# Square root and reciprocal for the first two layer-norm chunks, second halves on Pool, two weight loads on ScalarE's queue, staged warming

## The chip, the cores and the metric

The kernel runs on one core of a Trainium2 chip. The metric is device time in microseconds (us); lower is better. "Span" is the time from the first to the last instruction in a profile; it is about 1.8 us under the time. The engines are named as the profile names them: PE is TensorE's matmuls, PEld its weight loads, DVE is VectorE, ACT is ScalarE, POOL is GpSimd, SP is the engine that issues most DMAs.

## The reference, cut to what matters

```python
x  = A_x                                  # 2048 tokens x 1024, bf16
xn = layernorm(x)                         # over the 1024 columns
out = x + attention(xn, wq, wk, wv, wo, beta) + mixer(xn, w1, b1, w2, b2)

def mixer(x, w1, b1, w2, b2):
    h = layernorm(x)                      # a second norm, of the normed x
    u = gelu(einsum('bsd,sf->bdf', h, w1) + b1)   # contraction over the 2048 tokens
    ...
```

The first matmuls of the mixer contract over tokens. So the kernel can start them as soon as the first 128 tokens ("chunk 0" of 16) are loaded, normed and scaled. This document is about the first 8 us, up to there, and about how the following chunks keep up.

## The kernel before: the parts that matter

Names used below: `xin` is x as loaded, by chunk; `ln_st`, `ln_mv`, `ln_rs` hold statistics, mean and variance, and 1/std; `h` is the scaled chunk; `w1early` is the part of w1 that the first stage uses. Loads are all issued by SP, in this order (x chunks and w1 chunks: first chunk, count):

```python
for kind, c0, n in (("x", 0, 1), ("x", 1, 1), ("x", 2, 1), ("w", 0, 2), ("x", 3, 1), ("x", 4, 2), ("w", 2, 2), ("x", 6, 2),
                    ("w", 4, 4), ...):
    ...
with fw.group(reads=[self.R_warm], writes=[self.R_bank[0]]):
    for _ in range(self.N_WARM):          # 10 matmuls on zeros, to warm TensorE up
        fw.mm(self.bank(0), self.warm[:, 0:P], self.warm[:], start=True, stop=True)
```

Even chunks get their statistics on VectorE (`D`, `d`), odd ones on ScalarE (`A`, second pass `A'`). `S` is 1/std: an add of eps on VectorE, then a power of -0.5 on Pool. `h` is the scaling. This list is the order of emission; each engine runs its own part of it in order.

```python
NORM_ORDER = (["D0 A1 S0 d2 h0 A1' A3 S1 d2' h1"] +
              [f"S{c} d{c + 2} h{c} A{c + 1}' A{c + 3} S{c + 1} d{c + 2}' h{c + 1}" for c in range(2, 14, 2)] + ...)

def rstd(self, c):                        # S
    fw.op("dve", lambda e: e.tensor_scalar(var, ..., E_H, op0=ALU.mult, op1=ALU.add), ...)
    fw.op("pool", lambda e: e.tensor_tensor(rs, var, self.expo[:, 0:1], op=ALU.pow), ...)

def scale_h(self, c):                     # h: chunks 0 and 1 in two halves
    for h0, h1 in ((0, 1), (1, 2)) if c < 2 else ((0, 2),):
        cols = slice(512 * h0, 512 * h1)
        self.fw.op("dve", lambda e: e.tensor_scalar(self.h[:, c, cols], self.xin[:, c, cols], self.ln_mv[:, c, 0:1],
                                                    self.ln_rs[:, c, 1:2], op0=ALU.subtract, op1=ALU.mult), ...)
```

The first stage then runs 8 matmuls per chunk: 4 that need only the first half of h, then 4 that need the second half.

The softmax here doesn't subtract the row's maximum and nothing guards it: scores larger than these inputs give would overflow.

Of the kernel before, what the change touches and what calls it, by code (L numbers as in the profile page):

```python
# [6 lines left out]
ACT = mybir.ActivationFunctionType  # L7
# [338 lines left out]
class _Kernel:  # L346
# [31 lines left out]
    def alloc(self):  # L378
        nc = self.nc
        a = self.keep = _Arena(nc, self.SB_BASE, self.SB_END)  # L380
        self.ident = a.take("ident", [P, P], BF16)
        self.brow1 = a.take("brow1", [P, 32], BF16)
        self.brow2 = a.take("brow2", [P, 32], BF16)
        self.bcol = a.take("bcol", [P, 2, 32], BF16)
        self.b1c = a.take("b1c", [P, N_FCH], F32)
        self.b2c = a.take("b2c", [P, N_TCH], F32)
        self.beta_sb = a.take("beta_sb", [P, N_HEAD], BF16)
        self.gcol = a.take("gcol", [P, N_HEAD], F32)
        self.gate = a.take("gate", [P, N_GRP, 2, 4], F32)
        self.eps8 = a.take("eps8", [P, 2, 4], F32)  # L390
        self.diag = a.take("diag", [P, 4, VW], F32)
        self.ln_st = a.take("ln_st", [P, N_TCH, 12], F32)
        self.ln_mv = a.take("ln_mv", [P, N_TCH, 2], F32)
        self.ln_rs = a.take("ln_rs", [P, N_TCH, 2], F32)
        self.expo = a.take("expo", [P, N_TCH], F32)
        self.ln_sm = a.take("ln_sm", [P, N_TCH, 1], F32)
        self.vA = [a.take(f"vA{i}", [P, 4, 16, VW], BF16) for i in range(2)]
        self.MZ32 = a.take("MZ32", [P, N_GRP, GW], F32)
        self.MZbf = a.take("MZbf", [P, N_GRP, GW], BF16)
        self.srec = a.take("srec", [P, 2, 32], F32)  # L400
        self.xnT = [a.take(f"xnT{s}", [P, N_DCH, SEG_L], BF16) for s in range(N_SEG)]
        self.gT = a.take("gT", [P, N_FCH, D_MODEL], BF16)

        self.R_ident, self.R_beta, self.R_gcol, self.R_gate = Res("ident"), Res("beta"), Res("gcol"), Res("gate")
        self.R_brow1, self.R_brow2 = [[Res(f"brow{i}_{j}") for j in range(5)] for i in range(2)]
        self.R_b1c, self.R_b2c = Res("b1c"), Res("b2c")
        self.R_eps, self.R_diag = Res("eps8"), Res("diag")
        self.R_st = [Res(f"st{c}") for c in range(N_TCH)]
        self.R_rs = [Res(f"rs{c}") for c in range(N_TCH)]
        self.R_rs0, self.R_expo = Res("rs0"), Res("expo")  # L410
        self.R_vA = [[Res(f"vA{i}_{c}") for c in range(4)] for i in range(2)]
        self.R_MZ32 = [Res(f"mz32_{g}") for g in range(N_GRP)]
        self.R_MZbf = [Res(f"mzbf_{g}") for g in range(N_GRP)]
        self.R_srec = [Res(f"srec{i}") for i in range(2)]
        self.R_xnT = [Res(f"xnT{c}") for c in range(N_TCH)]
        self.R_gT = [[Res(f"gT{fc}_{h}") for h in range(2)] for fc in range(N_FCH)]
        self.R_out = [Res(f"out{c}") for c in range(N_TCH)]

        self.early_base = a.at
        e = _Arena(nc, self.early_base, self.SB_END)  # L420
        self.xin = e.take("xin", [P, N_TCH, D_MODEL], BF16)
        self.junk = e.take("junk", [P, D_MODEL], BF16)
        self.warm = e.take("warm", [P, 512], BF16)
        self.early_end = e.at = self.early_base + 40960
        self.h = e.take("h", [P, N_TCH, D_MODEL], BF16)
        w1_at = (e.at + 31) // 32 * 32
        self.w1ring = [e.take(f"w1s{i}", [P, N_TCH, 256], BF16) for i in range(3)]
        self.w1early = nc.alloc_sbuf_tensor_at("w1early", [P, N_TCH, 512], BF16, offset=w1_at)
        self.late_end = e.at
        self.R_xin = [Res(f"xin{c}") for c in range(N_TCH)]  # L430
        self.R_junk, self.R_warm = Res("junk"), Res("warm")
        self.R_h = [[Res(f"h{c}_{h}") for h in range(2)] for c in range(N_TCH)]
        self.R_hh = [[self.R_h[c][h] for c in range(N_TCH)] for h in range(2)]
        self.R_w1s = [Res(f"w1s{i}") for i in range(3)]
# [78 lines left out]
    def consts(self):  # L513
# [5 lines left out]
        for fp in range(N_FCH // 2):  # L519
            self.w1_ring.srcs.append(self.B_w1[:, fp * 256:(fp + 1) * 256].rearrange("(c p) f -> p c f", p=P))  # L520
        self.R_w1e = [Res(f"w1e{c}") for c in range(N_TCH)]
        fw.op("act", lambda e: e.activation(self.junk[:, 0:1], self.warm[:, 0:1], ACT.Gelu_apprx_tanh),
              reads=[self.R_warm], writes=[self.R_junk])
        for kind, c0, n in (("x", 0, 1), ("x", 1, 1), ("x", 2, 1), ("w", 0, 2), ("x", 3, 1), ("x", 4, 2), ("w", 2, 2), ("x", 6, 2),
                            ("w", 4, 4), ("x", 8, 4), ("w", 8, 4), ("x", 12, 4), ("w", 12, 4)):
            if kind == "x":
                self.load_x(c0, n)
            else:
                self.fw.dma(self.w1early[:, c0:c0 + n, :],
                            self.B_w1[c0 * P:(c0 + n) * P, 0:512].rearrange("(c p) f -> p c f", p=P),  # L530
                            writes=self.R_w1e[c0:c0 + n])
        self.w1_ring.issued = 2
        for brow, src, n, R in ((self.brow1, self.B_b1, N_FCH, self.R_brow1), (self.brow2, self.B_b2, N_TCH, self.R_brow2)):
            for j in range(4):
# [1 line left out]
                       reads=[R[4]], writes=[R[j]])  # L536
        fw.dma(self.beta_sb[:], self.A_beta.partition_broadcast(P), writes=[self.R_beta])

        fw.op("pool", lambda e: e.memset(self.expo[:], -0.5), writes=[self.R_expo])
        fw.op("pool", lambda e: e.memset(self.ident[:], 0.0), writes=[self.R_ident])  # L540
        fw.op("pool", lambda e: e.affine_select(self.ident[:], self.ident[:], pattern=[[-1, P]],
                                                compare_op=ALU.not_equal, fill=1.0, base=0,
                                                channel_multiplier=1),
              reads=[self.R_ident], writes=[self.R_ident])
        with fw.group(reads=[self.R_warm], writes=[self.R_bank[0]]):
            for _ in range(self.N_WARM):
                fw.mm(self.bank(0), self.warm[:, 0:P], self.warm[:], start=True, stop=True)

    def bias_columns(self):
# [22 lines left out]
    def gates(self):  # L572
# [13 lines left out]



    NORM_ORDER = (["D0 A1 S0 d2 h0 A1' A3 S1 d2' h1"] +
                  [f"S{c} d{c + 2} h{c} A{c + 1}' A{c + 3} S{c + 1} d{c + 2}' h{c + 1}" for c in range(2, 14, 2)] +  # L590
                  ["S14 h14 A15' S15 C h15"])

    def norm_and_first_hidden(self):
        for word in " ".join(self.NORM_ORDER).split():
            kind, second = word[0], word.endswith("'")
            c = int(word[1:].rstrip("'") or 0)
            if kind == "C":
                self.bias_columns()
            elif kind in "Dd":
                self.stats_dve(c, (0, 1) if kind == "D" else (1,) if second else (0,))  # L600
            elif kind == "A":
                self.stats_act(c, second)
            elif kind == "S":
                self.rstd(c)
            else:
                self.scale_h(c)
        self.rstd_first()
        for c in range(N_TCH - 2):
            self.early_hidden(c, c + 1, (range(0, 8, 2), range(1, 8, 2)))
        self.early_hidden(N_TCH - 2, N_TCH, [(b,) for b in range(8)])  # L610
        self.late_consts()

    def stats_dve(self, c, halves):
        fw = self.fw
        src, st, R = self.xin[:, c, :], self.ln_st[:, c, :], self.R_st[c]
        for h in halves:
            fw.op("dve", lambda e: e.bn_stats(st[:, 6 * h:6 * h + 6], src[:, 512 * h:512 * h + 512]),  # L617
                  reads=[self.R_xin[c]], writes=[R])
        if halves[-1]:
            fw.op("dve", lambda e: e.bn_aggr(self.ln_mv[:, c, :], st.rearrange("p (a s) -> p a s", s=6)),  # L620
                  reads=[R], writes=[R])

    def stats_act(self, c, second):

# [9 lines left out]
    def rstd(self, c):  # L634


        fw = self.fw
        R, var, rs = self.R_st[c], self.ln_mv[:, c, 1:2], self.ln_rs[:, c, 1:2]
        fw.op("dve", lambda e: e.tensor_scalar(var, self.ln_sm[:, c, :] if c % 2 else var, 1.0 / D_MODEL if c % 2 else 1.0,
                                               E_H, op0=ALU.mult, op1=ALU.add), reads=[R], writes=[R])  # L640
        fw.op("pool", lambda e: e.tensor_tensor(rs, var, self.expo[:, 0:1], op=ALU.pow), reads=[R, self.R_expo],
              writes=[self.R_rs[c]])

    def rstd_first(self):
        fw = self.fw
# [6 lines left out]
    def scale_h(self, c):  # L652
        reads = [self.R_xin[c], self.R_st[c], self.R_rs[c]]
        for h0, h1 in ((0, 1), (1, 2)) if c < 2 else ((0, 2),):
            cols = slice(512 * h0, 512 * h1)
            self.fw.op("dve", lambda e: e.tensor_scalar(self.h[:, c, cols], self.xin[:, c, cols], self.ln_mv[:, c, 0:1],
                                                        self.ln_rs[:, c, 1:2], op0=ALU.subtract, op1=ALU.mult),
                       reads=reads, writes=self.R_h[c][h0:h1])

    def early_hidden(self, c0, c1, bank_groups):  # L660
# [433 lines left out]
```

## Time and profile before

| | before |
|---|---|
| time, first three executions | 699.26, 697.68, 697.30 (median 697.68) |
| span of the profiled execution | 695.4 us |
| PE busy | 99% |
| first real matmul | 7.09 us |
| second stage starts | 34.71 us |

First, the page's busy times by engine, and its chain of what ended last:

```profile
PE 685.7 (99%) x4746; PEld 326.5 (47%) x4830; DVE 257.2 (37%) x581; ACT 277.7 (40%) x333; POOL 100.4 (14%) x156
PE 97%; DMA 1%; issue 1%; SPq 1%; DVE 0%
```

TensorE is the limit from end to end. Where it waits, the next view shows: the waits of PE (who waited for whom: us in total, times, longest).

```profile
PE ps_all L194 <- DVE h L656: 1.4, 1, 1.4
PE ps_all L194 <- DVE brow L517: 1.3, 1, 1.3
PE ps_all L194 <- issue: 0.3, 2, 0.2
```

There are two waits that matter, both in the first 7.1 us: before the warming matmuls, and between them and the first real one. The timeline of the head (start, duration, engine, line, operation, output and inputs, count, idle time before it and who ended it):

```profile
1.25 4.45 PE L194 MATMUL ps_all<-warm 128*128 128x512 bf16 x10 [1.25 <-DVE brow L517]
4.19 1.06 ACT L627 ACTIVATE junk<-xin 128x1024 bf16<-128x1024 bf16 x1 [1.89 <-DMA xin<-in_A_x_dram]
5.29 0.15 DVE L639 TENSOR_SCALAR ln_mv<-ln_mv 128x1 f32<-128x1 f32 x1
5.53 0.55 POOL L641 TENSOR_TENSOR ln_rs<-ln_mv,expo 128x1 f32<-128x1 f32 x1 [3.96 <-DVE ln_mv L639]
5.94 0.69 DVE L617 BATCH_NORM_STATS2 ln_st<-xin 128x6 f32<-128x512 bf16 x1 [0.49 <-DMA xin<-in_A_x_dram]
6.55 0.72 DVE L656 TENSOR_SCALAR h<-xin,ln_mv,ln_rs 128x512 bf16<-128x512 bf16 x2
7.09 27.79 PE L194 MATMUL ps_all<-h,w1early 128*128 128x512 bf16 x126 [1.39 <-DVE h L656]
34.71 5.56 PE L194 MATMUL ps_all<-h,w1s 128*128 128x512 bf16 x24
```

From 7.09 to 34.71 the 128 matmuls of the first stage take 27.62 us, 0.216 us each, without a gap. (The trace misses two of their records.)

A matmul's displayed end is modelled, about 0.38 us after its start, so a displayed idle time is some 0.16 us shorter than the time lost.

### The profile page before, as it was taken

To read this page: it belongs to the slowest core of one execution; us is meant where nothing else is said; L and a number is where in the kernel's file an instruction comes from. 1 tells how busy PE (TensorE), PEld (TensorE's weight loads), DVE (VectorE), ACT (ScalarE), POOL (GpSimd) and SP (SyncE) were. 2 spreads that over 40 slices of the span, in tenths; PEclk is the share of its full clock that TensorE was granted. 3 is DMA by queue.
4 is the path that set the end of the run, shared out by engine and by line. 5 is a ranking of instruction groups with operands and counts; after the bars stand their busy time and mean duration, and the time that the engine had idled before them with its cause. 6 is when DMAs were issued, how large, how long until landed. Compare 5 with 4: busy or idle time off the path is not lost.

```text
span 695.4 us, 11228 instructions
## 1 busy us (share of the span) xinstructions
PE 685.7 (99%) x4746; PEld 326.5 (47%) x4830; DVE 257.2 (37%) x581; ACT 277.7 (40%) x333; POOL 100.4 (14%) x156
## 2 busy tenths in 40 slices
PE   8999999999999999999999999999999999999998
PEld 3444444444444444444444445444444444445454
DVE  7740000000011334333436455536445553434445
ACT  7521211111134444444455444454544444534440
POOL 2600000000001111111121211112121111121130
PEclk9999999999999999999999999999999999999999
DMA  9497684227036536645263544525273544437014
GB/s 315 110 218 175 151 224 123 77 60 140 1 133 121 109 67 131 115 109 126 47 129 95 117 95 90 129 47 137 64 150 80 97 95 73 97 64 152 9 31 137
DMA packets 210537, 77.17 MB, mean 111 GB/s; under 512 B 173112, under 2 KB 202808, under 8 KB 210488
## 3 DMA queue, kind: packets, MB, share of 16 engines
q1 hardware_dynamic: 210344, 76.42, 47.8%
q8 instruction: 38, 0.62, 0.4%
q14 instruction: 11, 0.09, 0.1%
q10 hardware_dynamic: 144, 0.03, 0.0%
HBM read 59.79 MB, written 5.24 MB: 94 GB/s over the span
## 4 chain that ended last, share of the span: by engine, by line
PE 97%; DMA 1%; issue 1%; SPq 1%; DVE 0%
PE ps_all L194 97%; DMA xin<-in_A_x_dram 1%; SPq L216 1%; DVE ln_st L617 0%; DVE fin L1051 0%; PE ps_all L200 0%
## 5 line engine op out<-in xcount | busy, mean ns | idle before, releaser
L194 PE MATMUL ps_all<-gT,w2h 128*128 128x512 bf16 x868 | 207.8, 380 | 1.6 <-issue 0.2
L811 ACT ACTIVATE pT<-ps_all 128x512 bf16<-128x512 f32 (+1 forms) x128 | 151.4, 1234 | 76.7 <-PE ps_all L194 76.7
L194 PE MATMUL ps_all<-h,w1s 128*128 128x512 bf16 x752 | 165.1, 379 | 0.8
L806 POOL TENSOR_SCALAR_AFFINE_SELECT pT<-pT 128x512 bf16<-128x512 bf16 x128 | 83.9, 680 | 557.5 <-ACT pT L811 557.5
L194 PEld LDWEIGHTS ps_all<-gT,w2h 128*128 128x128 bf16 x896 | 83.1, 98 | 105.7 <-issue 13.8
L194 PEld LDWEIGHTS ps_all<-h,w1s 128*128 128x128 bf16 x768 | 75.1, 98 | 90.6
L845 DVE CAST ost<-ps_all 128x264 bf16<-128x264 f32 (+1 forms) x128 | 49.2, 398 | 169.4 <-PE ps_all L194 169.3
L713 ACT ACTIVATE gT<-ps_all,b1c 128x512 bf16<-128x512 f32 x56 | 35.1, 687 | 142.0 <-PE ps_all L194 136.4
L755 DVE CAST kT<-ps_all 128x512 bf16<-128x512 f32 x32 | 22.0, 688 | 176.9 <-PE ps_all L194 176.9
L194 PE MATMUL ps_all<-xnT,wk 128*128 128x512 bf16 x256 | 60.5, 379 | 0.0
L194 PE MATMUL ps_all<-xnT,wq 128*128 128x512 bf16 x256 | 60.4, 378 | 0.0
L194 PEld LDWEIGHTS ps_all<-vA,pT 128*128 128x128 bf16 x1280 | 47.7, 96 | 22.6
L194 PE MATMUL ps_all<-wv_sb,xnT 128*128 128x512 bf16 x227 | 54.0, 379 | 1.6
L739 ACT ACTIVATE qT<-ps_all 128x512 bf16<-128x512 f32 x32 | 19.1, 597 | 77.8 <-PE ps_all L194 77.8
L194 PE MATMUL ps_all<-vA,pT 128*128 128x33 bf16 x1280 | 48.6, 178 | 0.0
L951 DVE SCALAR_TENSOR_TENSOR stg<-ps_all,b2c,stg 128x512 bf16<-128x512 f32 x32 | 24.0, 750 | 61.7 <-PE ps_all L194 61.6
L758 ACT ACTIVATE etmp<-kT 128x512 bf16<-128x512 bf16 x24 | 15.1, 629 | 59.0 <-DVE kT L755 59.0
L194 PEld LDWEIGHTS ps_all<-xnT,wk 128*128 128x128 bf16 x256 | 23.8, 98 | 23.1
L194 PEld LDWEIGHTS ps_all<-wv_sb,xnT 128*128 128x128 bf16 x256 | 23.5, 97 | 23.7
L194 PEld LDWEIGHTS ps_all<-xnT,wq 128*128 128x128 bf16 x256 | 23.4, 97 | 23.2
L773 ACT ACTIVATE vA<-ps_all 128x512 bf16<-128x512 f32 x32 | 19.2, 600 | 37.1 <-PE ps_all L194 37.1
L194 PE MATMUL ps_all<-qT,kT 32*128 32x384 bf16 (+3 forms) x512 | 31.9, 299 | 0.0
(70 smaller groups left out, 419.7 us busy)
## 6 DMA issues: line engine op xcount, KB each, us to landing
w2h<-in_B_w_dram SPq DMA_DIRECT2D x32, 448.0 KB, 4.8
w1s<-in_B_w_dram SPq DMA_DIRECT2D x12, 1024.0 KB, 5.8
wq<-in_A_wq_dram SPq DMA_DIRECT2D x32, 256.0 KB, 4.4
wk<-in_A_wk_dram SPq DMA_DIRECT2D x32, 256.0 KB, 5.1
stg<-in_A_x_dram SPq DMA_DIRECT2D x16, 256.0 KB, 3.0
out_dram<-stg SPq DMA_DIRECT2D x16, 256.0 KB, 2.0
xin<-in_A_x_dram SPq DMA_DIRECT2D x2, 1024.0 KB, 10.5
wv_sb<-in_A_wv_dram SPq DMA_DIRECT2D x2, 1024.0 KB, 9.0
```

What stands on the lines that cost most here:

```text
L194: ins = self.nc.tensor.matmul(*args, **kwargs)
L216: ins = es.eng.dma_start(out_ap, in_ap, transpose=True) if transpose else es.eng.dma_start(out_ap, in_ap)
L713: fw.op("act", lambda e: e.activation(self.gT[:, fc, half * 512:(half + 1) * 512], self.bank(b), ACT.Gelu_apprx_tanh, bias=self.b1c[:, fc: ...
L739: fw.op("act", lambda e: e.activation(self.qT[k][:], self.bank(b), ACT.Copy), reads=[self.R_bank[b]], writes=[self.R_qT[k]])
L755: fw.op("dve", lambda e: e.tensor_copy(self.kT[k][:], self.bank(b)), reads=[self.R_bank[b]], writes=[self.R_kT[k]])
L758: fw.op("act", lambda e: e.activation(self.etmp[1][:], self.kT[k][:], ACT.Exp), reads=[self.R_kT[k]], writes=[self.R_etmp[1]])
L773: fw.op("act", lambda e: e.activation(self.vA[i][:, c, :, 0:D_HEAD], self.bank(b).rearrange("p (h d) -> p h d", d=D_HEAD), ACT.Copy), read ...
L806: fw.op("pool", lambda e: e.affine_select(d, d, pattern=[[0, 4], [1, P]], compare_op=ALU.is_ge, fill=0.0, base=0, channel_multiplier=-1), ...
L811: self.fw.op("act", lambda e: e.activation(dst, src, ACT.Exp, scale=SCALE), reads=R_src, writes=R_dst)
L845: fw.op("dve", lambda e: e.tensor_copy(dst, self.ps[:, b, 0:n * VW]), reads=[self.R_bank[b]], writes=[self.R_ost[o][qb]])
L951: fw.op("dve", lambda e: e.scalar_tensor_tensor(dst, self.bank(b), self.b2c[:, c:c + 1], dst, op0=ALU.add, op1=ALU.add), reads=[self.R_ban ...
```

## The change

The intent is an earlier first real matmul. Chunks 0 and 1 get their 1/std by a square root on ScalarE and a reciprocal on VectorE, in place of add and Pool power. VectorE scales only their first halves; Pool takes the second halves. The first two w1 loads go out on ScalarE's queue, early. Three more warming matmuls, which wait for chunk 0's statistics, fill TensorE's idle gap. The gelu table is loaded later, in ScalarE's idle time.

```diff
-        (activation of Gelu_apprx_tanh, to load its table)
+        self.load_table(ACT.Sqrt)
-        for kind, c0, n in (("x", 0, 1), ("x", 1, 1), ("x", 2, 1), ("w", 0, 2), ("x", 3, 1), ("x", 4, 2), ("w", 2, 2), ("x", 6, 2),
+        for kind, c0, n in (("x", 0, 1), ("x", 1, 1), ("w", 0, 2), ("x", 2, 1), ("w", 2, 2), ("x", 3, 1), ("x", 4, 2),
...
-                            writes=self.R_w1e[c0:c0 + n])
+                            writes=self.R_w1e[c0:c0 + n], issuer="act" if c0 < 4 else "sp")
...
-    NORM_ORDER = (["D0 A1 S0 d2 h0 A1' A3 S1 d2' h1"] +
+    NORM_ORDER = (["D0 W0 A1 Q0 r0 h0 A1' Q1 A3 d2 e2 r1 h1 g2 S2 d4 h2 A3' A5 S3 d4' h3 V0 V1"] +
...                  # W: keep_warm(3, [R_st[c]])   Q: square root   r: reciprocal
...                  # e, g: second half of the statistics, aggregate   V: the add of eps, late   G: gelu's table
+    def std_first(self, c):
+        ... "act", activation(self.ln_rs[:, c, 1:2], src, ACT.Sqrt, bias=self.e_h[:], scale=k)
+    def rstd_of_std(self, c):
+        ... "dve", reciprocal(rs, rs)
...
-            self.fw.op("dve", lambda e: e.tensor_scalar(self.h[:, c, cols], ...
+            self.fw.op("pool" if h0 else "dve",
+                       lambda e: e.tensor_scalar(self.h[:, c, cols], ...
```

More of the change, by code (lines that the diff above doesn't have):

```diff
@@ L395, in alloc @@
         self.expo = a.take("expo", [P, N_TCH], F32)
+        self.e_h = a.take("e_h", [P, 1], F32)
         self.ln_sm = a.take("ln_sm", [P, N_TCH, 1], F32)
@@ L521, in consts @@
         self.R_w1e = [Res(f"w1e{c}") for c in range(N_TCH)]
-        fw.op("act", lambda e: e.activation(self.junk[:, 0:1], self.warm[:, 0:1], ACT.Gelu_apprx_tanh),
-              reads=[self.R_warm], writes=[self.R_junk])
-        for kind, c0, n in (("x", 0, 1), ("x", 1, 1), ("x", 2, 1), ("w", 0, 2), ("x", 3, 1), ("x", 4, 2), ("w", 2, 2), ("x", 6, 2),
-                            ("w", 4, 4), ("x", 8, 4), ("w", 8, 4), ("x", 12, 4), ("w", 12, 4)):
+        self.load_table(ACT.Sqrt)
+        for kind, c0, n in (("x", 0, 1), ("x", 1, 1), ("w", 0, 2), ("x", 2, 1), ("w", 2, 2), ("x", 3, 1), ("x", 4, 2),
+                            ("x", 6, 2), ("w", 4, 4), ("x", 8, 4), ("w", 8, 4), ("x", 12, 4), ("w", 12, 4)):
             if kind == "x":
@@ L537, in consts @@
         fw.dma(self.beta_sb[:], self.A_beta.partition_broadcast(P), writes=[self.R_beta])
-        fw.op("pool", lambda e: e.memset(self.expo[:], -0.5), writes=[self.R_expo])
+        fw.op("pool", lambda e: e.memset(self.e_h[:], E_H), writes=[self.R_expo])
+        fw.op("pool", lambda e: e.memset(self.expo[:], -0.5), reads=[self.R_expo], writes=[self.R_expo])
         fw.op("pool", lambda e: e.memset(self.ident[:], 0.0), writes=[self.R_ident])
@@ L544, in consts, with load_table, keep_warm @@
               reads=[self.R_ident], writes=[self.R_ident])
-        with fw.group(reads=[self.R_warm], writes=[self.R_bank[0]]):
-            for _ in range(self.N_WARM):
+        self.keep_warm(self.N_WARM)
+    def load_table(self, func):
+        self.fw.op("act", lambda e: e.activation(self.junk[:, 0:1], self.warm[:, 0:1], func), reads=[self.R_warm],
+                   writes=[self.R_junk])
+    def keep_warm(self, n, reads=()):
+        fw = self.fw
+        with fw.group(reads=[self.R_warm, *reads], writes=[self.R_bank[0]]):
+            for _ in range(n):
                 fw.mm(self.bank(0), self.warm[:, 0:P], self.warm[:], start=True, stop=True)
@@ L584, in gates @@
               reads=[self.R_gcol, self.R_gate], writes=[self.R_gate])
-    NORM_ORDER = (["D0 A1 S0 d2 h0 A1' A3 S1 d2' h1"] +
-                  [f"S{c} d{c + 2} h{c} A{c + 1}' A{c + 3} S{c + 1} d{c + 2}' h{c + 1}" for c in range(2, 14, 2)] +
-                  ["S14 h14 A15' S15 C h15"])
+    NORM_ORDER = (["D0 W0 A1 Q0 r0 h0 A1' Q1 A3 d2 e2 r1 h1 g2 S2 d4 h2 A3' A5 S3 d4' h3 V0 V1"] +
+                  [f"S{c} d{c + 2} h{c} A{c + 1}' A{c + 3} S{c + 1} d{c + 2}' h{c + 1}" for c in range(4, 14, 2)] +
+                  ["S14 h14 A15' G S15 C h15"])
     def norm_and_first_hidden(self):
@@ L598, in norm_and_first_hidden @@
                 self.bias_columns()
+            elif kind == "W":
+                self.keep_warm(3, [self.R_st[c]])
             elif kind in "Dd":
                 self.stats_dve(c, (0, 1) if kind == "D" else (1,) if second else (0,))
+            elif kind == "e":
+                self.stats_dve(c, (1,), False)
+            elif kind == "g":
+                self.stats_sum(c)
+            elif kind == "Q":
+                self.std_first(c)
+            elif kind == "r":
+                self.rstd_of_std(c)
+            elif kind == "V":
+                self.add_e_h(c)
+            elif kind == "G":
+                self.load_table(ACT.Gelu_apprx_tanh)
             elif kind == "A":
@@ L611, in norm_and_first_hidden, with stats_dve @@
         self.late_consts()
-    def stats_dve(self, c, halves):
+    def stats_dve(self, c, halves, sum_up=True):
         fw = self.fw
@@ L618, in stats_dve, with stats_sum @@
                   reads=[self.R_xin[c]], writes=[R])
-        if halves[-1]:
-            fw.op("dve", lambda e: e.bn_aggr(self.ln_mv[:, c, :], st.rearrange("p (a s) -> p a s", s=6)),
-                  reads=[R], writes=[R])
+        if halves[-1] and sum_up:
+            self.stats_sum(c)
+    def stats_sum(self, c):
+        st, R = self.ln_st[:, c, :], self.R_st[c]
+        self.fw.op("dve", lambda e: e.bn_aggr(self.ln_mv[:, c, :], st.rearrange("p (a s) -> p a s", s=6)),
+                   reads=[R], writes=[R])
     def stats_act(self, c, second):
@@ L634, in rstd, with add_e_h @@
     def rstd(self, c):
-        fw = self.fw
-        R, var, rs = self.R_st[c], self.ln_mv[:, c, 1:2], self.ln_rs[:, c, 1:2]
-        fw.op("dve", lambda e: e.tensor_scalar(var, self.ln_sm[:, c, :] if c % 2 else var, 1.0 / D_MODEL if c % 2 else 1.0,
-                                               E_H, op0=ALU.mult, op1=ALU.add), reads=[R], writes=[R])
-        fw.op("pool", lambda e: e.tensor_tensor(rs, var, self.expo[:, 0:1], op=ALU.pow), reads=[R, self.R_expo],
-              writes=[self.R_rs[c]])
+        self.add_e_h(c)
+        self.fw.op("pool", lambda e: e.tensor_tensor(self.ln_rs[:, c, 1:2], self.ln_mv[:, c, 1:2], self.expo[:, 0:1],
+                                                     op=ALU.pow), reads=[self.R_st[c], self.R_expo], writes=[self.R_rs[c]])
+    def add_e_h(self, c):
+        var = self.ln_mv[:, c, 1:2]
+        self.fw.op("dve", lambda e: e.tensor_scalar(var, self.ln_sm[:, c, :] if c % 2 else var,
+                                                    1.0 / D_MODEL if c % 2 else 1.0, E_H, op0=ALU.mult, op1=ALU.add),
+                   reads=[self.R_st[c]], writes=[self.R_st[c]])
+    def std_first(self, c):
+        src, k = (self.ln_sm[:, c, :], 1.0 / D_MODEL) if c % 2 else (self.ln_mv[:, c, 1:2], 1.0)
+        self.fw.op("act", lambda e: e.activation(self.ln_rs[:, c, 1:2], src, ACT.Sqrt, bias=self.e_h[:], scale=k),
+                   reads=[self.R_st[c], self.R_expo], writes=[self.R_rs[c]])
+    def rstd_of_std(self, c):
+        rs = self.ln_rs[:, c, 1:2]
+        self.fw.op("dve", lambda e: e.reciprocal(rs, rs), reads=[self.R_rs[c]], writes=[self.R_rs[c]])
     def rstd_first(self):
@@ L655, in scale_h @@
             cols = slice(512 * h0, 512 * h1)
-            self.fw.op("dve", lambda e: e.tensor_scalar(self.h[:, c, cols], self.xin[:, c, cols], self.ln_mv[:, c, 0:1],
-                                                        self.ln_rs[:, c, 1:2], op0=ALU.subtract, op1=ALU.mult),
+            self.fw.op("pool" if h0 else "dve",
+                       lambda e: e.tensor_scalar(self.h[:, c, cols], self.xin[:, c, cols], self.ln_mv[:, c, 0:1],
+                                                 self.ln_rs[:, c, 1:2], op0=ALU.subtract, op1=ALU.mult),
                        reads=reads, writes=self.R_h[c][h0:h1])
```

## The prediction

> **What bounds it now.** TensorE. The page has PE busy 99% of a 695.4 us span; the chain of waits is 97% matmuls. By the waits of PE, its only idle time is at the head: 1.3 us before the warming matmuls and 1.4 us between them and the first real matmul (released by the h write); all later waits sum to 0.3 us. In the timeline the first real matmul starts at 7.09, the first stage's 128 take 27.6 us (0.216 us each), and steady stretches have the same pitch: no stall. Granted clock 1.0. So the change, which touches only the head and the layer norm under the first stage, can win at most what it moves that first matmul forward, and loses whatever later chunks then make PE wait.
>
> **The chain to 7.09 (timeline).** x chunk 0 lands 3.55; two halves of statistics to 5.01; aggregate to 5.26; add eps 5.29-5.44; Pool power 5.53-6.08; VectorE, in order, is in chunk 2's statistics 5.94-6.63 (it waited for x2), so h0 runs from 6.55 and PE starts 7.09. The first w1 load, issued 2.19 with 4.5 us to landing, arrives about 6.7, hardly earlier.
>
> **What changes.** Chunk 0: out go the add (0.15), the power (0.55), about 0.2 of handovers and some 0.47 behind chunk 2; in come a ScalarE square root (estimate 0.25-0.3 from the 0.20 us one-column activation plus 0.09 for a bias column, by 1148 against 1056 ns) and a reciprocal (0.15). ScalarE is in chunk 1's mean until 5.34, so: root 5.4-5.65, reciprocal to 5.85, h0's first half to 6.25, PE about 6.35. Potential: 0.7 us. Pool's second halves (estimate 0.7, as its 680 ns select) have 0.86 us of first-half matmuls to hide under.
> The square-root table replaces the gelu table at the start (1.28 us); gelu's load moves to about 25 us, where ScalarE idles 7.1 us: free.
>
> **What eats it.** (1) ScalarE can issue its w1 loads at about 1.3-2.3, ahead of x2. The Trainium skill, "DMA: Bandwidth & Descriptors", section "Issuing engines are not separate DMA queues", says that they interleave on the same 16 DMA engines; this trace shows 350-380 GB/s from 2.5 us on, i.e. full. So w1 lands earlier, but x1 (4.15 now) later by up to 0.7 us; that delays ScalarE's mean of chunk 1 and the root queued behind it. (2) Three more warming matmuls sit ahead of the first real one, after chunk 0's statistics. At today's warming pitch of 0.427 us (half rate) PE is occupied to about 6.8; at full pitch to 6.2. The skill, "TensorE: Matmul & The Clock Gate", Part 1, says the rate rises after about 3.4 us of a free-running window; this trace shows half rate through the tenth at 5.1 and full at 7.09. (3) VectorE's h1, h2, h4 then have 0-0.3 us of slack against PE's 1.73 us a chunk; x8 landing at 14.95 puts h6 at 16.1, needed at 16.7. Small stalls are possible.
>
> I expect the first real matmul near 6.7 and 0.1 us of new stalls: net gain about 0.3 us. The runs before spread over 2 us (697.3 to 699.26), so noise decides most of the range. Predicted **697.3 us**, range **696.2 to 698.5**; faster by over 2% 0.005, within 2% 0.99, slower by over 2% 0.005.
>
> **Right or wrong in the profile.** First real matmul 6.3-6.9; PE waits in 7-35 us under 0.3 us in sum; gelu table load in ScalarE's idle time near 25 us; root about 5.4 (or 6, if x1 is late); everything after 35 us the same, shifted.
>
> **What would make it wrong.** x1 so late that PE starts at 7.2 or later; PE still at half rate in its first real matmuls (0.2 us lost each); Pool's half blocked or over 1 us; VectorE's order starving h1 or h2; different luck in the runs.

## The result, and the profile after

| | before | after |
|---|---|---|
| median of 6 executions | 697.53 | 698.96 |
| lowest, highest | 697.14, 699.26 | 698.57, 699.53 |
| span of the profiled execution | 695.4 | 697.1 |
| first real matmul | 7.09 | 7.04 |
| second stage starts | 34.71 | 36.44 |
| lost in the first stage | 0 | 1.78 |

The ratio of after to before is 1.0015, with a 95% interval of 1.0002 to 1.0028. A ratio here is the mean time of one kernel's fast runs over that of the other's of the same rounds, so it is not quite the ratio of the medians. By the 2% rule this is "same", and yet it is a loss clear of noise, outside the predicted range.

The second stage starts 1.73 us later, and the span is 1.7 us longer. All of the difference is in the first stage. **What the first stage loses = (start of the second stage - first real matmul) - 27.62 us**. The waits of PE in the kernel after:

```profile
PE ps_all L194 <- DVE brow L518: 1.3, 1, 1.3
PE ps_all L194 <- POOL h L697: 1.0, 2, 0.8
PE ps_all L194 <- DVE h L697: 1.0, 1, 1.0
PE ps_all L194 <- DVE ln_mv L671: 0.2, 1, 0.2
```

Two waits for Pool and the last one, for VectorE, are new. (The profile puts the last one down to `ln_mv`; by its times it ends with chunk 2's `h`, which runs from 11.58.) The timeline of the head after:

```profile
4.92 1.06 ACT L655 ACTIVATE junk<-xin 128x1024 bf16<-128x1024 bf16 x1 [2.61 <-DMA xin<-in_A_x_dram]
5.97 0.28 ACT L677 ACTIVATE ln_rs<-ln_mv,e_h 128x1 f32<-128x1 f32 x1
6.28 0.17 DVE L682 RECIPROCAL ln_rs<-ln_rs 128x1 f32<-128x1 f32 x1 [1.10 <-ACT ln_rs L677]
6.48 0.41 DVE L697 TENSOR_SCALAR h<-xin,ln_mv,ln_rs 128x512 bf16<-128x512 bf16 x1
6.64 4.29 POOL L697 TENSOR_SCALAR h<-xin,ln_mv,ln_rs 128x512 bf16<-128x512 bf16 x2 [4.91 <-DVE ln_rs L682]
7.04 1.02 PE L194 MATMUL ps_all<-h,w1early 128*128 128x512 bf16 x4 [0.98 <-DVE h L697]
8.90 1.90 PE L194 MATMUL ps_all<-h,w1early 128*128 128x512 bf16 x8 [0.84 <-POOL h L697]
10.90 0.56 POOL L666 TENSOR_TENSOR ln_rs<-ln_mv,expo 128x1 f32<-128x1 f32 x1
10.99 1.04 PE L194 MATMUL ps_all<-h,w1early 128*128 128x512 bf16 x4 [0.18 <-POOL h L697]
11.58 0.55 DVE L697 TENSOR_SCALAR h<-xin,ln_mv,ln_rs 128x1024 bf16<-128x1024 bf16 x1 [1.68 <-POOL ln_rs L666]
12.27 24.33 PE L194 MATMUL ps_all<-h,w1early 128*128 128x512 bf16 x110 [0.24 <-DVE ln_mv L671]
```

Read down the PE lines. After 4 matmuls (0.86 us at 0.216) PE could go on at 7.90, and goes on at 8.90, when Pool has chunk 0's second half ready. After 8 more it could go on at 10.63, and goes on at 10.99, when Pool has chunk 1's. After 4 more, at 11.85, it waits for chunk 2 until 12.27: Pool, which works in order, could compute chunk 2's power only at 10.90, behind its second half. That is 1.00 + 0.36 + 0.42 = 1.78 us. Pool's two halves took 4.29 us together; the prediction had put 0.7 us on one.

The ScalarE line at 4.92 is the second thing to see. x1's first use came 0.73 us later than before (4.19), where ScalarE had waited for the load. The square root stood behind that work, so the first real matmul came at 7.04 and nearly nothing was won at the start.

### The profile page after: what moved, and what is told of

Same layout as the page of the kernel before. It is cut to its first block, busy times and chain, and to the rows that moved or that the text cites. A ratio compares the mean times of both kernels' runs of the same rounds, so it can differ in the third digit from the quotient of the medians.

```text
span 697.1 us, 11240 instructions
## 1 busy us (share of the span) xinstructions
PE 686.7 (98%) x4749; PEld 326.4 (47%) x4833; DVE 257.2 (37%) x581; ACT 279.3 (40%) x337; POOL 103.4 (15%) x157
## 4 chain that ended last, share of the span: by engine, by line
PE 97%; issue 1%; POOL 1%; DMA 1%; DVE 0%; ACT 0%; SPq 0%; DVEq 0%; POOLq 0%
PE ps_all L194 97%; POOL h L697 1%; DMA xin<-in_A_x_dram 1%; DVE h L697 0%; POOL ln_rs L666 0%; SPq L216 0%; DVE fin L1092 0%; PE ps_all L200 0%; ACT junk L655 0%; ACT ln_rs L677 0%; DVE ln_rs L682 0%; DVE ln_mv L671 0%; DVEq L69 0%; POOLq L69 0%
```

## The experiments

The theory at this point, called P: Pool's halves cost the time, directly and through the power behind them. Rivals: L, the reordered loads cost it; Q, the square root. Later a question came up that no theory had covered, why executions of the kernel before spread over almost 3 us; its theory is called C, for the clock.

The table holds all runs (there is no e6 on record): first real matmul, start of the second stage and loss in the first stage are from the one profiled execution; the times are from all of that kernel's executions.

| run | first matmul | 2nd stage | lost | median | lowest to highest |
|---|---|---|---|---|---|
| before (36 executions, on three chips or more) | 7.09 | 34.71 | 0 | | 696.61 to 699.47 |
| after (6) | 7.04 | 36.44 | 1.78 | 698.96 | 698.57 to 699.53 |
| e13, after again (5) | 6.70 | 36.30 | 1.98 | 698.95 | 698.74 to 699.00 |
| e1, halves on VectorE (4) | 6.77 | 35.74 | 1.35 | 698.21 | 697.55 to 698.34 |
| e3, Pool only for chunk 0 (4) | 6.73 | 35.37 | 1.02 | 697.84 | 697.76 to 698.64 |
| e14, after with old loads (5) | 6.46 | 35.87 | 1.79 | 698.34 | 698.17 to 698.44 |
| e4, before with a test of Pool's instruction (1) | 6.74 | 36.05 | 1.69 | 698.49 | one execution |
| e5, VectorE halves and old loads (4) | 6.75 | 34.73 | 0.36 | 697.21 | 697.09 to 697.27 |
| e12, e5 without staged warming (5) | 6.77 | 34.56 | 0.17 | 697.13 | 696.96 to 697.34 |
| e2, before with Pool halves (4) | 7.21 | 36.59 | 1.76 | 699.14 | 698.95 to 700.71 |
| e15, before with new loads (6) | 7.36 | 36.58 | 1.60 | 699.78 | 699.00 to 701.46 |
| e7, before with staged warming (6) | 7.71 | 35.33 | 0.00 | 697.99 | 697.71 to 698.63 |
| e10, the same, mended (5) | 6.92 | 34.54 | 0.00 | 697.11 | 696.81 to 697.55 |
| e9, before with 6 warming matmuls (6) | 6.71 | 36.02 | 1.69 | 698.64 | 698.46 to 700.35 |
| e8, candidate (6) | 6.31 | 35.48 | 1.55 | 697.58 | 697.10 to 697.92 |
| e11, second candidate (6) | 6.35 | 35.37 | 1.40 | 697.74 | 697.20 to 697.91 |

e13 is the changed kernel once more; 698.6 to 699.5 was expected, and it repeats the result.

### e1: all halves back on VectorE

```diff
-            self.fw.op("pool" if h0 else "dve",
+            self.fw.op("dve",
```

> The changed kernel with all halves of h back on VectorE; roots, loads and warming stay changed. Theory P (Pool's halves, 2.1-2.2 us each, are what cost the time, directly and by holding up chunk 2's power behind them): of the 1.78 us of PE stalls in the first stage some 1.1 go, the rest (0.5-0.7) stays, because VectorE's order puts both halves of chunk 2's statistics ahead of h1; first real matmul still 7.04, time about 697.9, i.e. 1.0 us under the changed kernel. Rival L (the reordered loads, with x1 0.7 us later, cost it): the stalls stay near 1.8 us and the time near 699.0. Rival Q (square root instead of power): the same as L.

Measured: 698.21, against 698.95 of the changed kernel; ratio to before 1.0001 (0.9981 to 1.0021). The waits for Pool are gone, and 0.7 us with them. But the first stage still lost 1.35 us, about twice what theory P had left over. The profile names the reason. First VectorE, then PE:

```profile
7.56 1.42 DVE L641 BATCH_NORM_STATS2 ln_st<-xin 128x6 f32<-128x512 bf16 x2 [0.81 <-DMA xin<-in_A_x_dram]
9.09 0.74 DVE L697 TENSOR_SCALAR h<-xin,ln_mv,ln_rs 128x512 bf16<-128x512 bf16 x2
9.55 26.35 PE L194 MATMUL ps_all<-h,w1early 128*128 128x512 bf16 x118 [0.79 <-DVE h L697]
```

VectorE waited for x2 until 7.56; before, x2 was there at 5.94. The new order puts both halves of chunk 2's statistics (1.42 us) ahead of chunk 1's scaling, so chunk 1 came at 9.09 and PE waited. Pool was one loss. The loads and the order were another, which Pool's wait had covered. How late x2 comes under the new loads varies from one execution to the next: VectorE's wait for it ended at 6.92 in e13, 6.95 in e3 and 7.56 here. So 1.35 us is what this execution lost, and not a fixed price.

### e3: Pool only for chunk 0

```diff
-            self.fw.op("pool" if h0 else "dve",
+            self.fw.op("pool" if h0 and c == 0 else "dve",
```

> The changed kernel with Pool scaling only the second half of chunk 0; chunk 1's is back on VectorE. Theory P with its knock-on: the wait for h0's half stays (about 1.0 us of pitch), the waits for h1's half (0.36) and for chunk 2 (0.42, its power queued behind Pool until 10.90) go; first stage ends 0.7-0.8 us sooner, time about 698.2. If the knock-on is wrong, only the 0.36 goes and chunk 2's wait stays.

Measured: a loss of 1.02 us for 1.78, as expected; the time, 697.84, came out 0.4 under the 698.2 expected, with the first matmul at 6.73 in the profiled execution. The wait for chunk 0's half stayed (0.84 displayed, 1.00 in pitch). The waits for chunk 1's half and for chunk 2 went. In the profile the power of chunk 2 ran at 9.60, not at 10.90. So the knock-on through Pool's order is shown:

```profile
9.60 0.57 POOL L666 TENSOR_TENSOR ln_rs<-ln_mv,expo 128x1 f32<-128x1 f32 x1 [1.06 <-DVE ln_mv L671]
```

### e4: what Pool's instruction costs by itself

Extra instructions were put at about 62 us, where Pool and VectorE idle and PE does not wait for them. They do not touch the result.

```diff
+            if fc == 8:
+                self.bench(fc)       # Pool: (x - a) * b over 512, 256, 1024; with constants; one product; copy;
+                                     # then the 512 form again beside twelve of VectorE's own
```

> The kernel before with a few extra instructions on Pool and VectorE at about 62 us, where both are idle and TensorE does not wait for them: Pool's (x - mean) * rstd with two per-partition columns over 512, 256 and 1024 elements, the same over 512 with two constants, a product with one constant, a copy; then the 512 form once more while VectorE runs twelve of its own. Theory I (the operation is slow by itself on Pool): 2.0-2.2 us for 512 alone, about half for 256, twice for 1024. Rival S (it was slow because VectorE's scaling and statistics shared its way to the memory): 0.6-0.9 us alone, about 2 us beside VectorE. Time as before.

The groups of instructions by form in that stretch, on Pool and then on VectorE (count, busy us, mean ns of one, idle time before):

```profile
L719 POOL TENSOR_SCALAR junk<-h,ln_mv,ln_rs 128x512 bf16<-128x512 bf16 x2 | 4.4, 2210 | 30.1 <-ACT gT L738 29.9
L719 POOL TENSOR_SCALAR junk<-h,ln_mv,ln_rs 128x1024 bf16<-128x1024 bf16 x1 | 3.8, 3780 | 0.1
L719 POOL TENSOR_SCALAR junk<-h 128x512 bf16<-128x512 bf16 x1 | 1.9, 1922 | 0.1
L725 POOL TENSOR_SCALAR junk<-h 128x512 bf16<-128x512 bf16 x1 | 1.5, 1504 | 0.1
L719 POOL TENSOR_SCALAR junk<-h,ln_mv,ln_rs 128x256 bf16<-128x256 bf16 x1 | 1.2, 1218 | 0.1
L727 POOL COPY junk<-h 128x512 bf16<-128x512 bf16 x1 | 0.6, 609 | 0.1
L719 DVE TENSOR_SCALAR warm<-h,ln_mv,ln_rs 128x512 bf16<-128x512 bf16 x1 | 0.4, 413 | 23.2 <-ACT gT L738 23.2
```

The scaling of 512 columns takes 2.2 us on Pool, alone (65.25 to 67.46) just as beside VectorE, and 0.41 us on VectorE. Its cost grows with the columns: 1.22, 2.21, 3.78 us for 256, 512, 1024. It hangs on the arithmetic, too: a copy of the same size takes 0.61 us, one product 1.50, two operations 1.92. So the instruction is slow by itself (theory I); a fight with VectorE did not make it slow (rival S falls). The next Pool instruction started 2.31 us after the first (65.25, 67.55), so the length is not an artefact of how the profile marks an end. What misled the prediction was borrowing the 680 ns of another Pool instruction, the select, which has the same shape. The page of the kernel before has it (count, busy us, mean ns of one, idle time before):

```profile
L806 POOL TENSOR_SCALAR_AFFINE_SELECT pT<-pT 128x512 bf16<-128x512 bf16 x128 | 83.9, 680 | 557.5 <-ACT pT L811 557.5
```

Run once, this kernel took 698.49. Its head is that of before, with a different fate; see theory C below.

### e5 and e14: the loads put back, without and with Pool's halves

```diff
-        for kind, c0, n in (("x", 0, 1), ("x", 1, 1), ("w", 0, 2), ("x", 2, 1), ("w", 2, 2), ("x", 3, 1), ...
+        for kind, c0, n in (("x", 0, 1), ("x", 1, 1), ("x", 2, 1), ("w", 0, 2), ("x", 3, 1), ("x", 4, 2), ("w", 2, 2), ...
-                            ..., issuer="act" if c0 < 4 else "sp")
+                            ..., issuer="sp")
```

e5 has this and the halves on VectorE:

> All halves on VectorE and the loads as in the kernel before (one queue, old order); square roots, VectorE's new order and staged warming stay. x1 lands again at 4.15 (4.88 in the changed kernel), root at 5.4 instead of 5.97, h0's first half done by 6.3; the first w1 load lands about 6.7 and becomes what PE waits for: first real matmul about 6.8, then 0.3-0.5 us of stalls at h1 and h2. Time about 697.7, between this and the run with new loads there should be 0.2-0.4 us. Rival L says that the loads were the loss, and sees 1 us or more.

e14 has this alone; Pool keeps its halves:

> The changed kernel with nothing but its loads put back (one queue, old order); Pool's halves stay. If the two losses hide one another (each covers the other's wait), as the traces suggest: first real matmul 6.75, Pool's h0 half ready at 8.0-8.1 (0.5 us of stall), h1's at 10.2 (0.4), chunk 2 behind the power at 10.8 (0.4): 1.3 us of stalls, about 698.2. If Pool alone is the loss: 699. If the loads alone are: 697.3.

e5 measured 697.21 and lost 0.36 us in the first stage. That is as expected for the head (first matmul 6.75, x1 at 4.31, root at 5.38), but the step from e1 to e5 is 1.0 us, not the 0.2 to 0.4 expected. That part of the expectation missed: in these two traces it is x2's lateness, not x1's, that the loads cost. VectorE took chunk 2's statistics at 6.56 without a wait (7.56 in e1), and PE ran on:

```profile
6.56 1.42 DVE L641 BATCH_NORM_STATS2 ln_st<-xin 128x6 f32<-128x512 bf16 x2
6.75 28.14 PE L194 MATMUL ps_all<-h,w1early 128*128 128x512 bf16 x126
```

So of rival L a part holds.

e14 measured 698.34 (expected: about 698.2, by a start at 6.75 and stalls of 1.3 us; it started earlier and lost more, so part of that agreement is luck). Its PE lines:

```profile
6.46 1.02 PE L194 MATMUL ps_all<-h,w1early 128*128 128x512 bf16 x4
8.33 1.90 PE L194 MATMUL ps_all<-h,w1early 128*128 128x512 bf16 x8 [0.84 <-POOL h L697]
10.41 1.04 PE L194 MATMUL ps_all<-h,w1early 128*128 128x512 bf16 x4 [0.18 <-POOL h L697]
11.70 24.33 PE L194 MATMUL ps_all<-h,w1early 128*128 128x512 bf16 x110 [0.25 <-DVE ln_mv L671]
```

The pattern of the changed kernel, 0.58 us earlier, and the same loss of 1.79 us. So while Pool's halves stay, the old loads win only the earlier start. Starting from the changed kernel's 36.44, the second stage starts 0.70 us earlier without Pool's halves, 0.57 earlier with the old loads, and 1.71 earlier with both. The two losses cover one another: taking one away leaves PE waiting for the other. One profiled execution stands behind each of these numbers, and the start alone varied by 0.34 us between two executions of the changed kernel (7.04, 6.70); the medians say the same: 698.96 and 698.95 with both, 698.21 and 698.34 with one, 697.21 with neither.

In e5 the square roots stay, and e5 is no slower than before's good executions (697.2): rival Q falls.

### e2: only Pool's halves, on the kernel before

```diff
-            self.fw.op("dve", lambda e: e.tensor_scalar(self.h[:, c, cols], ...
+            self.fw.op("pool" if h0 else "dve", lambda e: e.tensor_scalar(self.h[:, c, cols], ...
```

> The kernel before with only the second halves of h0 and h1 moved to Pool; it still has the power on Pool, the old loads and warming. Theory P: Pool 2.1-2.2 us per half; chunk 1's power queues behind h0's half (ready 7.3, starts 8.8), so h1 comes at 9.5 instead of 8.1; PE stalls of 2.5 to 4 us in the first stage and a time of 700 to 701.5. Rivals L and Q: no stall beyond 0.3 us, 697.5.

Measured: 699.14 (698.95 to 700.71). Slower, as theory P says, but under the 700 to 701.5 expected, and the trace does not show it in the way expected: after the first real matmul PE waited for nobody, and the stage lost 1.76 us all the same. Its first nine real matmuls ran at half rate, one every 0.427 us. At that rate PE was slow enough for Pool to keep up. So this run could not weigh Pool's halves; it showed that something else goes on at the head.

### Theory C: when TensorE goes to full rate

Warming matmuls run one every 0.427 us, half rate. The Trainium skill, "TensorE: Matmul & The Clock Gate", Part 1, says that TensorE starts at half rate and goes to full rate after a busy window of about 3.4 us, and that the window is free-running, so that the moment differs from run to run. That the moment differs these traces show: full rate came at about 4.1 us (e3), 5.0 (after) and 7.0 (e1), and PE was busy from 1.25 on in all three. The length they do not quite bear out: in e3 the rate rose 2.9 us after the first matmul, in less than 3.4. But in e2, e4, e9 and e15 it came only at 10 to 10.7. What those have in common is an idle gap between warming and real matmuls and no staged warming, as in the kernel before. But before's own trace and e12's have that too, and run at full rate from their first real matmul or soon after.

In the timeline half rate is seen best on the weight loads (PEld): while PE is slow, each of them idles 0.28 us first. Here e9, from the first real matmul on:

```profile
6.68 0.14 PEld L194 LDWEIGHTS ps_all<-h,w1early 128*128 128x128 bf16 x2 [3.59 <-DMA w1early<-in_B_w_dram]
7.09 0.15 PEld L194 LDWEIGHTS ps_all<-h,w1early 128*128 128x128 bf16 x1 [0.28 <-issue]
7.52 0.15 PEld L194 LDWEIGHTS ps_all<-h,w1early 128*128 128x128 bf16 x1 [0.28 <-issue]
...
9.65 0.15 PEld L194 LDWEIGHTS ps_all<-h,w1early 128*128 128x128 bf16 x1 [0.28 <-DVE ln_st L617]
10.08 5.96 PEld L194 LDWEIGHTS ps_all<-h,w1early 128*128 128x128 bf16 x28 [0.28 <-issue]
```

And the clock that the profile prints does not show it here. These are e9's cores view, and its busy times by stretch of 2 us (length; busy time and count of PE, PEld, DVE, ACT, POOL; granted clock; DMA share; GB/s):

```profile
core 0: 696.7 us, clock 1.000
7.00:9.00 2.00, 2.00 (x6) 0.73 (x5) 1.69 (x6) 1.55 (x3) 1.02 (x2) 1.00 1.03 367
11.00:13.00 2.00, 2.00 (x11) 0.94 (x10) 1.86 (x6) 1.88 (x4) 0.78 (x2) 1.00 1.05 375
```

6 matmuls started in one stretch and 11 in the other, PE busy all the time in both, the clock given as 1.00 in both. e9's page has no clock row at all, nor have those of e2, e4, e14 and e15, though e14 ran at full rate from its first real matmul on (6.46). So the 1.00 goes with a missing record and measures nothing here. In before, whose page has the row, the view gives 1.00 for 1 to 3 us too, where the warming runs at half rate. Count matmuls per us at the head; do not trust the clock there.

**e9: fewer warming matmuls, and so a longer gap.**

```diff
-    N_WARM = 10
+    N_WARM = 6
```

> The kernel before with 6 warming matmuls for 10, so that the idle gap before the first real one is 3.3 us for 1.6. Theory C: nearly every execution has its first real matmuls at half rate, which costs 1 to 2.5 us: 698.5 to 700. Rival H: as before.

All six executions were slow, 698.46 to 700.35, as theory C expects. The first real matmul came no later than before (6.71), and the stage lost 1.69 us to half rate alone. But the edit changed two things, the gap and the warming itself, from 4.3 us to 2.6 (10 and 6 matmuls at 0.427). A rival to the gap is left untested: that PE must have been busy long enough before it. Two traces favour this rival. e7 (below) idled 1.57 us before its first real matmul and ran at full rate at once, while e4 idled 1.05 and did not; e7's matmuls had reached the full rate before the gap, e4's had not. So a gap of that length by itself is not the cause.

**e7 and e10: the staged warming alone, on the kernel before.** The first try waited for chunk 0's statistics in the ordinary way; the second one without being recorded as their reader.

```diff
-    NORM_ORDER = (["D0 A1 S0 d2 h0 ...
+    NORM_ORDER = (["D0 W0 A1 S0 d2 h0 ...
+            elif kind == "W":        # e7: reads=[self.R_warm, self.R_st[c]]; e10: extra=[self.R_st[c].w]
+                with self.fw.group(...): 3 warming matmuls
```

> The kernel before plus nothing but the staged warming (three more warming matmuls that wait for chunk 0's statistics). Theory C (the runs of before spread over 696.6 to 699.5 because the idle gap from 5.5 to 7.1 lets the moment at which TensorE goes to full rate come late, or lets it fall back, in some executions): first real matmul about 7.0-7.1 as before, all executions within 0.5 us of each other near 697.3, none with a granted clock under 1.0; the mean falls by 0.4-0.8 us. Rival H (spread comes from elsewhere): the spread stays 2-3 us and the mean unchanged.

e7 failed as an experiment. VectorE's add of eps writes what the warming matmuls were recorded as reading, so it waited for their end (6.25, before 5.29), and the first real matmul came at 7.71. The change itself has that add, `V0 V1`, after h3, out of the way of this wait. The spread of e7, 0.9 us, is over the 0.5 that theory C expected, and under the 2 to 3 of rival H.

> The kernel before plus the staged warming alone, this time waiting for chunk 0's statistics without being recorded as their reader (in the earlier try VectorE's add of eps had to wait for the warming matmuls to end, 6.25 instead of 5.3). Theory C: first real matmul at 7.0-7.1, all executions 697.0 to 697.7, mean 0.3 to 0.8 us under that of before, whose executions spread from 696.6 to 699.5. Rival H (the spread has another source): spread and mean as before.

e10: 696.81 to 697.55, first real matmul 6.92, nothing lost. Before, in the same rounds on the same chip: 696.86 to 699.32, with 3 of 11 executions over 698.4. The mean fell from 697.57 to 697.16, the ratio is 0.9996 (0.9984 to 1.0008), so a difference is not shown, though no slow execution occurred.

**e12: e5 without its staged warming.**

```diff
-    NORM_ORDER = (["D0 W0 A1 Q0 r0 h0 ...
+    NORM_ORDER = (["D0 A1 Q0 r0 h0 ...
```

> The run with VectorE's halves and the old loads (four executions within 0.2 us, 697.1 to 697.3), without its staged warming. Theory C: the spread comes back: a third to two thirds of the executions are 1 to 2.5 us slower than the rest, the best ones at 696.9-697.3. Rival H: all executions within 0.5 us again.

A miss for theory C: five executions, none slow (696.96 to 697.34). With 14 of 36 executions of before over 698.4, five good ones in a row would come with a chance of about 0.085 by luck. e12's gap, to 6.77, is 0.3 us shorter than before's, which may have helped; but e4 had its first real matmul at 6.74 after the same warming, and full rate came late in it. Five executions can't settle it.

The count over all runs: in kernels with staged warming, 51 executions, none with a granted clock under 1.0 and none with a spread over 1 us within a kernel. Without it and with a gap: before 14 of 36 over 698.4, with 5 granted clocks of 0.997 or 0.998 in the 30 executions whose clock is listed; e9 6 of 6 slow; e15 6 of 6 slow; e2 4 of 4 over 698.9, Pool's halves included; e12 0 of 5. Late full rate itself is shown by four traces, one each of e2, e4, e9 and e15; for the other executions counted here it is inferred from their times. The granted clock tells little: e9's six slow executions all have 1.0. What brings late full rate, the gap or too little busy time before it, is open, and so is how often it comes. No trace of before itself was taken in a slow execution, but e4's head is before's, instruction for instruction.

### e15: only the new loads, on the kernel before

```diff
+        (order of loads and issuer as in the change; nothing else)
```

> The kernel before with nothing but the new loads (first two w1 loads on ScalarE's queue, ahead of x2). x1 lands at 4.5-4.9 for 4.2, x2 at 6.9-7.6 for 5.9; VectorE takes chunk 2's statistics before h0, so h0 comes 0.9-1.5 us later: first real matmul 8.0-8.5 for 7.09, no big stall after it. Fast executions near 698.2; with the idle gap of 2.5 us more executions with a late full rate (700) than before has. If the loads are harmless by themselves: 697.2.

Measured: 699.00 to 701.46, ratio 1.0027 (1.0012 to 1.0041). x1 came late as expected (4.68), x2 only a little (6.21 for 5.94), so the first real matmul was at 7.36, not at 8.0 to 8.5. The rest is half rate: 1.60 us lost, full rate at about 10.6. A start 0.27 us later was the direct cost of the profiled execution, which also had the slow head. The times of the other five, none under 699.00, suggest the same.

### e8 and e11: looking for a version that beats both

Both take e5, put chunk 1's scaling ahead of the second half of chunk 2's statistics, scale chunk 2 in halves, and use two staged warming matmuls. They differ in the loads: x0, x1, w1 0-1, x2, x3, x4-5, w1 2-3 in e8; x0, x1, w1 0, x2, w1 1, x3, x4-5, w1 2-3 in e11.

> A candidate for better than both: the changed kernel with all halves on VectorE, all loads on one queue in the order x0, x1, w1 0-1, x2, x3, x4-5, w1 2-3, two staged warming matmuls for three, chunk 1's scaling ahead of the second half of chunk 2's statistics, and chunk 2 scaled in halves. Expected: first real matmul at 6.4-6.5 (6.75 with the old loads), then 0.4-0.5 us of stall at chunk 2, which VectorE cannot finish before 10.2; first stage ends about 34.5 against 34.7 before; time 697.0, spread under 0.5 us.

> The candidate mended: in the first one x2 came at 7.4 and w1's chunks 2-3 at 11.3, both waited for. Now w1's chunks 0 and 1 are loads of their own, one after x1 and one after x2, chunks 2-3 after x4-5; the rest as in the first candidate. Expected: first real matmul 6.4-6.5, x2 at 6.3-6.6, no wait at chunk 1, 0.5 us at chunk 2 (VectorE's limit), end of the first stage 34.5-34.6 against 34.7 before; executions 696.7 to 697.3.

Both started earlier than expected (6.31 and 6.35, for 6.4 to 6.5) and gave it all back. e8 waited for x2 until 7.44, and for w1 2-3 until 11.3. e11 waited for x4 until 10.04 (8.7 in e4 and e9), and again for w1 until 11.2; 0.43 of its 1.40 us went to half rate, which lasted to 7.2. In both, loads moved ahead put others behind, though not because the DMAs moved their most all the time: they moved 191 (e8) and 195 GB/s (e11) from 4 to 5 us, and 389 and 383 from 10 to 12. Times: 697.58 and 697.74, ratios 0.9993 (0.9978 to 1.0009) and 1.0003 (0.9991 to 1.0015). No run found a version that beats before's good executions (about 697.1). e5, e10 and e12 equal them, and none of the three showed its slow ones, in 14 executions.

## Why the prediction was wrong

The prediction said 697.3, with a range to 698.5. The measured time was 698.96.

- **"Pool's second halves (estimate 0.7, as its 680 ns select) have 0.86 us of first-half matmuls to hide under."** This is the step that failed first. The term was mis-sized: 2.21 and 2.09 us in the change, 2.21 alone in e4, so it could not hide. It made PE wait 1.00 + 0.36 us, and, since Pool also computes chunk 2's power and works in order, 0.42 us more. The prediction did name "Pool's half blocked or over 1 us" among what would make it wrong, but gave it no weight in the range.
- **"w1 lands earlier, but x1 (4.15 now) later by up to 0.7 us."** Right: x1's consumer started at 4.92 for 4.19, and at 4.58 in e13. That agrees with the page which the prediction cites, by which loads from two queues share the DMA engines. (The trace has 365 and 381 GB/s from 2.5 to 3.5 us, but 209 to 289 from 4.0 to 5.5.) But this is the second step that failed: the argument stopped at x1. x2 is delayed as well (7.56 in e1), and the changed order on VectorE makes chunk 1 wait for chunk 2's statistics. "Small stalls are possible", 0.1 us, was 1.35 us in e1, where Pool no longer covered it.
- **First real matmul near 6.7 (6.3 to 6.9).** 7.04 in the profiled execution, 6.70 in the second one. The latter is near by luck: the root ran at 5.63, not 5.4.
- **Three warming matmuls in the way, to 6.2 or 6.8.** Both kinds occur. In the changed kernel's profile they ran at full rate and cost nothing; in e1 they ran at half rate to the first real matmul at 6.77.
- **"The runs before spread over 2 us, so noise decides most of the range."** The spread was taken for noise. It has two groups, around 697.1 and around 698.8, and late full rate, seen in the trace of e4 with the same head, goes with the second. No execution with staged warming was slow in this way, but neither was one of e12, which has none. So the change may carry a gain in the mean, which no run shows apart from noise (e10); against before's good executions it loses about 1.8 us (698.95 to 697.1), which is what the traces show (1.73).
- **Right:** TensorE as the limit, and the size of the effect bounded by the head; root 0.28 us, reciprocal 0.17 us; root at about 6 if x1 is late (5.97); gelu's table load in ScalarE's idle time (25.01 us, 1.28 us); nothing changed after the first stage.

## What to carry to other kernels

Cost a moved instruction by its own operation on the new engine, measured in a spot where that engine idles; an instruction of the same shape but with other arithmetic can be a third of its price, and an in-order engine passes the delay on to whatever stands behind. When two waits run side by side, taking one away shows only the difference to the other, so undo the parts of a change alone and together. Where executions fall in two groups, count matmuls at the head to see at which rate TensorE ran, before calling it noise.

## What the Trainium skill lacked or had wrong

- "GPSIMD Engine Reference", section 4.1 "Engine selection": it advises VectorE for elementwise work, and calls operations with one input roughly line-rate on GpSimd. A copy of 128x512 bf16 comes nearest (0.61 us), but one product took 1.50 us, two operations with constants 1.92, and with two per-partition columns 2.21 (3.78 for 1024 columns), against 0.41 us on VectorE. Section 3.1 of the page has durations for other forms, none for this one.
- "TensorE: Matmul & The Clock Gate", Part 1, "HAM oscillation": it warns of idle gaps over about 3.4 us, for a TensorE that is at full rate already; the gap of 1.57 us in e7 agrees. It does not say what a shorter gap before the rise does: after 1.05 to 2.72 us of idle time between warming and work full rate came only at 10 to 10.7 us (e2, e4, e9, e15), with a loss of 1.6 to 1.8 us, though not in before (1.39) and e12 (1.07).
- "SBUF — State Buffer", "Who interferes with whom": it says that VectorE's scaling and a GpSimd instruction can exclude one another for a whole instruction. In e4 Pool's 2.21 us were unchanged beside VectorE, and VectorE completed four of its own in 2.43 us meanwhile (about 1.8 us at the pitch of 0.45 that it had after it): slowed, not blocked. The page says it of certain modes of VectorE; no run shows whether VectorE was in one.
- "TensorE: Matmul & The Clock Gate", Part 1, warns that the trace's events of the clock gate have been seen to be unreliable. It lacks that they can be missing altogether: five pages here have no clock row (e2, e4, e9, e14, e15), and the view reads 1.00 while TensorE starts a matmul every 0.427 us, as in e9's stretch from 7 to 9 us.
